# Decode attention over a key and value cache: values of pairs 0 to 12 issued by ScalarE instead of SyncE

## The chip, the core and the metric

The kernel runs on one core of a Trainium2 chip. The core has four engines that compute (TensorE or PE for matrix products, VectorE or DVE, ScalarE or ACT, GpSimd or POOL), SyncE (SP), which here only issues transfers, and 16 DMA engines that move data between the memory of the chip (HBM) and the memory of the core (SBUF, 128 partitions). Every engine works through its own list of instructions in order; semaphores tie the lists together. A transfer is issued by an instruction in the list of one engine, which puts it into that engine's DMA queue. The metric is the time of one execution on the device in microseconds (us), lower is better.

## The reference

One token is decoded. The cache holds 8192 keys and values for each of 32 heads, 128 numbers (float32) to a row, so that keys and values are 134 MB each.

```python
def _A_ref(x, k_cache, v_cache, wq, wo):            # x: [1, 1, 512]
    q = (x @ wq).reshape(B, Sq, H, Dh).transpose(0, 2, 1, 3)   # H = 32, Dh = 128
    scores = jnp.einsum("bhqd,bhkd->bhqk", q, k_cache) * (Dh ** -0.5)
    p = _softmax(scores, axis=-1)                   # over Sk = 8192
    o = jnp.einsum("bhqk,bhkd->bhqd", p, v_cache)
    return o.transpose(0, 2, 1, 3).reshape(B, Sq, H * Dh) @ wo
...
xn = _layernorm(x, axis=-1)
s = _A_ref(xn, A_k_cache, A_v_cache, A_wq, A_wo)
g = _silu(_B_ref(xn, B_w_gate, B_w_up, B_w_down))   # a gated layer, 512 -> 1376 -> 512
return x + s * g
```

## The kernel before

**Tiling.** The heads are worked in 16 pairs (`NP`). The keys of one pair are 8 MB and lie on 128 partitions, 64 for each head, as rows of 128 keys of 128 numbers (64 KB to a partition); the values likewise. SBUF holds three such slots: keys use `slots[0]` and `slots[1]` in turn (`slots[(i + 1) % 2]`), values always use `slots[2]`.

**One pair, in the order of its work.** VectorE multiplies the keys in place with the query of the head (L415) and sums each row (L416): these are the scores (`scores(i)`), and the step `summed[i]` marks their end. It then takes their largest (L418). TensorE turns these maxima to one row, VectorE reduces them (`all_max`, L408), TensorE spreads them, ScalarE makes the exponentials (`powers_of`, L428 and L430) and TensorE sums them. TensorE then multiplies weights and values in 64 matmuls (`pair`, L384 to L391) and raises `valued`; ScalarE copies the result out (`parts`, L437), TensorE picks the two heads from it and raises `picked`, and VectorE turns them (`heads_out`, L423).

**The loop over pairs (L440 to L458)** is written once per pair and fills the lists of all engines. VectorE's list holds, in this order, `all_max(i-1)`, `scores(i)`, `heads_out(i-1)`; ScalarE's holds `powers_of(i-1)`, `parts(i-1)`. TensorE runs `pair` in a loop, one pair after the other.

**Transfers.** All loads but one small one stand in SyncE's list, whose order is also the order of its DMA queue. `load_keys(i)` waits until VectorE has done the scores of pair i−2, which used the same slot (`summed[i - 2]`). `load_values(i - 1)` waits until TensorE has done the values of pair i−2 (`valued`). So SyncE's list reads K(2), V(1), K(3), V(2) and so on, with V(0) ahead of it, which waits for the end of the gated layer (`gated`). Each transfer of a full slot raises its own semaphore by 16 when it has landed. At the end SyncE's list has K(14), V(13), K(15), then the values of pairs 14 and 15 in parts, then the pieces of `wo`, which go to a key slot. The one load on ScalarE's queue is the row x (2 KB, L240).

**The end.** When the last pair is done, VectorE divides by the sums and turns the heads (`place`), and TensorE and VectorE share the product with `wo` (L507 to L539).

Of the kernel before, what the change touches and what calls it, by code (L numbers as in the profile page):

```python
# [51 lines left out]
def kernel(  # L52
# [19 lines left out]
    NP = H // 2  # L72
# [24 lines left out]
    DVE, ACT, SP, POOL = nc.vector, nc.scalar, nc.sync, nc.gpsimd  # L97
# [8 lines left out]
    def sb(name, *shape):  # L106
        return nc.alloc_sbuf_tensor(name, [P, *shape], F32)[:]
# [10 lines left out]
    slots = [sb(f"slot{i}", SLOT) for i in range(3)]  # L118
# [55 lines left out]
    def wait(eng, *steps):  # L174
        for s in steps:
            if s is not None:
                eng.wait_ge(*s)
# [24 lines left out]
    def rows_of(src, i):  # L202
        rows = src.rearrange("b h s d -> (b h s) d")[2 * i * S:2 * (i + 1) * S, :]
        return rows.rearrange("(p j) d -> p (j d)", p=P)
# [8 lines left out]
    def cols(j):  # L213
        return slice(j.start * Dh, j.stop * Dh)
# [5 lines left out]
            ld_k.setdefault(i, []).append((j, load(SP, f"k{n}_{j.start}", slots[n][:, cols(j)], rows_of(k_cache, i)[:, cols(j)])))  # L220

    def load_values(i, cut, *after):

        wait(SP, *after)
        for j in cut:
            sem = s_val[((0,) + V_CUTS).index(j.start)]
            SP.dma_start(slots[2][:, cols(j)], rows_of(v_cache, i)[:, cols(j)]).then_inc(sem, 16)  # L227

    load_keys(0, FULL)

# [138 lines left out]
    wait(PE, act(ACT.copy(s_gate, big[0])))  # L369
    gated = column_sums(big[1], s_gate)  # L370
    load_values(0, FULL, gated)
    wait(ACT, gated)
    c_sig = act(ACT.activation(g_row, big[1][:, :GC], AF.Sigmoid))
# [66 lines left out]
    for i in range(NP):  # L440
        if i > 0:
            all_max(i - 1)
        if i >= 2:
            load_keys(i, pieces(*K_CUTS.get(i, ())), summed[i - 2])
            if i < NP - 1:
                load_values(i - 1, FULL, (valued, i - 1))
        if i == NP - 1:
            for v, cut in ((i - 1, V_HALVES), (i, V_THREE)):
                load_values(v, cut[:1], (halved, v))
                load_values(v, cut[1:], (valued, v))  # L450
        scores(i)
        if i > 0:
            powers_of(i - 1)
            parts(i - 1)
            heads_out(i - 1)
        if i == 1:
            wait(DVE, c_sig)
            c_gate = dve(DVE.tensor_mul(g_row, g_row, big[1][:, :GC]))  # L458
# [81 lines left out]
    after = PE.take()  # L540
# [58 lines left out]
```

## Time and profile before

| | us |
|---|---|
| time, median of 3 runs | 684.8 (684.69 to 685.06) |
| the profiled execution's own time | 684.69 |
| its span, from the first to the last instruction | 683.3 |
| VectorE waited for keys, 8 times in all | 19.9 |
| keys, from issue to landing, median of the 13 full ones | 42.0 |
| values, from issue to landing, median of the 14 full ones | 29.3 |

The times of the views are those of the profiled execution, counted from the start of its span. In a row of the timeline the first number is the start and the second the length; then come engine, line, operation, what is written and read, and in brackets how long the engine had stood idle before and what ended that. A row of SPq or ACTq is an instruction that issues a transfer, so its length is that of the issue. The DMA view gives for each issue the time until the data had landed, and for each hardware queue its packets, its megabytes and its share of the time of 16 engines. In the windows view a row has, for each engine, busy time and number of instructions, then the granted clock of TensorE, the busy share of the DMA engines and GB/s. L38 stands for all instructions of TensorE, since a helper records them.

### The profile page before, as it was taken

How to read it: one execution, taken by the hardware profiler on the slowest of the kernel's cores; microseconds unless marked ns; L12 is line 12 of the kernel's file. 1: busy time of each engine (PE TensorE's matmuls, PEld its weight loads, DVE VectorE, ACT ScalarE, POOL GpSimd, SP SyncE). 2: the span in 40 equal slices, each digit the busy share in tenths (PEclk: the TensorE clock that was granted, in tenths of full speed). 3: DMA queues.
4: the chain of work that ended last, by engine and by line, in shares of the span. 5: the costliest groups of instructions: out<-in, count | busy, mean ns of one | idle time of the engine just before them, and what ended most of it. 6: DMA issues, size and time to landing. Idle time of an engine off the chain costs nothing. (4 is left out here: it accounts for less than half of the span.)

```text
span 683.3 us, 3400 instructions
## 1 busy us (share of the span) xinstructions
PE 218.8 (32%) x1376; PEld 62.3 (9%) x1376; DVE 616.0 (90%) x156; ACT 44.6 (7%) x142; POOL 2.6 (0%) x11
## 2 busy tenths in 40 slices
PE   0363025050503305050512306060512406060665
PEld 0120001010100101010100101010100101010110
DVE  3869999999999999998989899898989999999917
ACT  2040010000000100000010100000010101000010
POOL 0000000000000000000000000000000000000000
PEclk9987557575755757575665757575665757575897
DMA  9999999999999999999999999999999999999997
GB/s 382 429 440 460 437 434 430 430 430 430 430 430 430 430 430 430 460 441 445 434 430 430 430 430 430 430 430 430 430 437 437 460 430 403 472 399 430 435 430 331
DMA packets 7552, 293.67 MB, mean 430 GB/s; under 512 B 856, under 2 KB 864, under 8 KB 1664
## 3 DMA queue, kind: packets, MB, share of 16 engines
q1 hardware_dynamic: 7544, 293.67, 99.5%
q10 hardware_dynamic: 8, 0.00, 0.0%
HBM read 293.67 MB, written 0.00 MB: 430 GB/s over the span
## 5 line engine op out<-in xcount | busy, mean ns | idle before, releaser
L415 DVE TENSOR_TENSOR slot<-slot,q_all 128x16384 f32<-128x16384 f32 (+3 forms) x19 | 275.9, 14520 | 19.9 <-DMA slot<-in_A_k_cache_dram 19.9
L416 DVE TENSOR_REDUCE sc<-slot 128x128 f32<-128x16384 f32 (+3 forms) x19 | 276.0, 14525 | 0.7
L38 PE MATMUL psum<-slot,zeros 128*8 128x512 f32 x1024 | 148.5, 739 | 253.6 <-PEq L38 253.6
L38 PEld LDWEIGHTS psum<-slot,zeros 128*8 128x8 f32 x1024 | 30.3, 103 | 358.2 <-issue 358.2
L38 PE MATMUL psum<-ident,mx 128*1 128x128 f32 x32 | 8.4, 360 | 114.3 <-PEq L38 114.3
L437 ACT COPY o<-psum 128x512 f32<-128x512 f32 x16 | 9.4, 586 | 400.1 <-PE psum L38 400.1
L38 PE MATMUL psum<-slot,ones 128*128 (+3 forms) x36 | 17.7, 668 | 22.1 <-PEq L38 16.6
L290 DVE SCALAR_TENSOR_TENSOR slot<-slot,xn 128x1376 f32<-128x1376 f32 (+1 forms) x8 | 18.9, 2360 | 3.0 <-DMA slot<-in_A_wq_dram 2.7
L38 PE MATMUL psum<-o,pick 128*2 128x128 f32 x128 | 16.5, 272 | 12.8 <-PEq L38 12.8
L423 DVE STREAM_TRANSPOSE psum<-psum 32x128 f32<-32x128 f32 x16 | 5.0, 310 | 11.1 <-PE psum L38 11.1
L428 ACT ACTIVATE nb<-psum 128x2 f32<-128x2 f32 x16 | 2.8, 172 | 156.1 <-PE psum L38 156.1
L430 ACT ACTIVATE zeros<-sc,nb 64x128 f32<-64x128 f32 x32 | 12.8, 399 | 0.9
L38 PEld LDWEIGHTS psum<-ident,mx 128*1 128x1 f32 x32 | 1.8, 80 | 118.4 <-issue 118.3
L38 PEld LDWEIGHTS psum<-o,pick 128*2 128x2 f32 x128 | 9.9, 84 | 29.6 <-issue 27.2
L38 PE MATMUL psum<-slot,o_all 128*1 128x128 f32 (+1 forms) x54 | 9.5, 463 | 6.5 <-DMA slot<-in_A_wo_dram 6.5
L38 PE MATMUL psum<-zeros,rs 128*32 128x2 f32 x32 | 3.7, 187 | 23.5 <-PEq L38 23.5
L408 DVE TENSOR_REDUCE mx<-psum 1x2 f32<-1x128 f32 x16 | 4.4, 277 | 7.5 <-PE psum L38 7.5
L38 PE MATMUL psum<-mx,ones 1*128 1x2 f32 x32 | 8.2, 324 | 7.4 <-PEq L38 7.4
L515 DVE SCALAR_TENSOR_TENSOR q_all<-slot,o_all,q_all 128x512 f32<-128x512 f32 x15 | 10.0, 747 | 0.0
L38 PEld LDWEIGHTS psum<-slot,ones 128*128 128x128 f32 (+1 forms) x36 | 7.0, 218 | 32.5 <-issue 24.7
L38 PE MATMUL psum<-slot,o 128*1 128x512 f32 x26 | 5.0, 827 | 11.2 <-DMA slot<-in_B_w_down_dram 11.2
L38 PEld LDWEIGHTS psum<-mx,ones 1*128 1x128 f32 x32 | 7.3, 282 | 14.0 <-issue 14.0
(54 smaller groups left out, 61.3 us busy)
## 6 DMA issues: line engine op xcount, KB each, us to landing
slot<-in_A_k_cache_dram SPq DMA_DIRECT2D x2, 6144.0 KB, 37.9
slot<-in_A_v_cache_dram SPq DMA_DIRECT2D x3, 4096.0 KB, 23.0
slot<-in_A_wq_dram SPq DMA_DIRECT2D x2, 4096.0 KB, 16.6
slot<-in_A_k_cache_dram SPq DMA_DIRECT2D x2, 4096.0 KB, 40.5
slot<-in_A_k_cache_dram SPq DMA_DIRECT2D x2, 2048.0 KB, 42.4
slot<-in_B_w_gate_dram SPq DMA_DIRECT2D x1, 2752.0 KB, 26.9
slot<-in_B_w_up_dram SPq DMA_DIRECT2D x1, 2752.0 KB, 33.0
slot<-in_B_w_down_dram SPq DMA_DIRECT2D x1, 2560.0 KB, 22.7
```

What stands on the lines that cost most here:

```text
L38: ins = getattr(self.engine, name)(*args, **kwargs)
L290: return dve(DVE.scalar_tensor_tensor(y, w[:, k, cols], xn[:, k:k + 1], y, op0=ALU.mult, op1=ALU.add))
L408: DVE.reduce_max(mx[:1, 1:3], pt[0:1, :].rearrange("o (e p) -> o e p", e=2), axis=AX.X).then_inc(reduced, 1)
L415: wait(DVE, dve(DVE.tensor_mul(k[:, j, :], k[:, j, :], qb[:, i:i + 1, :].to_broadcast([P, n, Dh]))))
L416: summed[i] = dve(DVE.reduce_sum(sc[i % 2][:, j], k[:, j, :], axis=AX.X))
L423: turned_out[i] = dve(DVE.transpose(o, pn.rearrange("e (a r) -> e a r", r=WR)))
L428: wait(ACT, act(ACT.mul(nb, pm[:, :2], -SCALE)))
L430: ACT.activation(weights[h, :, e * HT:(e + 1) * HT], sc[i % 2][h].rearrange("p (g b) -> p g b", b=HT), AF.Exp, bias=nb[h, e:e + 1], scale= ...
L437: ACT.copy(o1, po).then_inc(copied, 1)
L515: ins = DVE.scalar_tensor_tensor(part[n], wo_t[:, r, :], col, part[n], op0=ALU.mult, op1=ALU.add)
```

## The change

The values of pairs 0 to 12 are issued by ScalarE, those of pairs 13 to 15 by SyncE as before. The waits are the same and move with the issues. In ScalarE's list the load of V(i−1) stands ahead of `powers_of(i-1)` and behind `parts(i-2)`; the first, V(0), stands ahead of the sigmoid of the gated layer (L373). SyncE's list keeps the keys, the weights and the end: K(2) to K(14) follow each other there with no values between them, then V(13), K(15) and the rest.

```diff
     def load_values(i, cut, *after):
-
-        wait(SP, *after)
+        eng = SP if i >= NP - 3 else ACT
+        wait(eng, *after)
         for j in cut:
             sem = s_val[((0,) + V_CUTS).index(j.start)]
-            SP.dma_start(slots[2][:, cols(j)], rows_of(v_cache, i)[:, cols(j)]).then_inc(sem, 16)
+            eng.dma_start(slots[2][:, cols(j)], rows_of(v_cache, i)[:, cols(j)]).then_inc(sem, 16)
```

## The prediction

> **What bounds the kernel now.** I read the page's header first, then its DMA lines, then the windows by stage.
>
> ```profile
> span 683.3 us, 3400 instructions
> DMA  9999999999999999999999999999999999999997
> q1 hardware_dynamic: 7544, 293.67, 99.5%
> 0.00:3.00 3.00, 0.00 (x0) 0.00 (x0) 0.17 (x1) 0.00 (x0) 0.99 (x8) 1.00 0.59 175
> 280.00:560.00 280.00, 80.31 (x546) 23.04 (x546) 258.93 (x37) 13.22 (x49) 0.00 (x0) 0.63 1.00 434
> ```
>
> The reader is to see that the 16 DMA engines, not VectorE, are the limit: one queue (q1, SP's) keeps them busy for 99.5% of the span, and the middle 280 us show a DMA share of 1.00 at 434 GB/s with VectorE at 259 of 280. So a change of order can gain almost nothing on the transfers; it can only lose, by leaving them without work. The question is what keeps them supplied. I write K(i) and V(i) for the loads of keys and values of pair i, S(i) for the end of its scores on VectorE, D(i) for the end of its value matmuls.
>
> ```profile
> 67.91 0.33 SPq L227 DMA_DIRECT2D slot<-in_A_v_cache_dram  x1
> slot<-in_A_v_cache_dram SPq DMA_DIRECT2D x1, 32.4
> 100.45 9.59 PE L38 MATMUL psum<-slot,zeros 128*8 128x512 f32 x64 [3.37 <-PEq L38]
> 370.97 9.15 PE L38 MATMUL psum<-slot,zeros 128*8 128x512 f32 x64 [20.01 <-PEq L38]
> 380.19 0.33 SPq L227 DMA_DIRECT2D slot<-in_A_v_cache_dram  x1
> 525.52 8.68 PE L38 MATMUL psum<-slot,zeros 128*8 128x512 f32 x64 [19.93 <-PEq L38]
> ```
>
> V(0), issued at 67.91, landed 32.4 later at 100.3; its matmuls start at 100.45. From there to those of pair 11 at 525.52 are 11 periods: 38.64 us each, two transfers of **19.32 us**. The values of pair 7 start at 370.97 and the next V, which waits for nothing else, is issued at 380.19: D is **9.2 us** after the landing's 0.1 (the whole group is 148.5 us for 16 pairs, 9.28).
>
> ```profile
> 312.87 17.23 DVE L415 TENSOR_TENSOR slot<-slot,q_all 128x16384 f32<-128x16384 f32 x1 [2.76 <-DMA slot<-in_A_k_cache_dram]
> 342.07 0.33 SPq L227 DMA_DIRECT2D slot<-in_A_v_cache_dram  x1
> slot<-in_A_v_cache_dram SPq DMA_DIRECT2D x1, 28.8
> 347.38 0.33 SPq L168 DMA_DIRECT2D slot<-in_A_k_cache_dram  x1
> slot<-in_A_k_cache_dram SPq DMA_DIRECT2D x1, 42.7
> ```
>
> Scores take 347.38 − 312.87 = **34.51 us**, and S(i) releases the slot for K(i+2), issued in the same instant. V lands 28.8 us after its issue: 9.5 us of waiting behind the K in transfer, then 19.3 at the full rate. That wait is the reserve. It covers the 9.2 us of matmuls in which the only value slot can take no load, and it exists because transfers are done whole, one after the other.
>
> **What the change does to each part.** Removed from SP: 13 value issues of 0.33 us and SP's waits for D. The K issues gain nothing by it: at 347.38 the K goes out with S(7) already now, and waits 23 us in its queue. The price of zero is covered by that. Added to ScalarE: 13 issues. The one issue that ScalarE makes before is the row of 1.08 us below; the SP row is 0.33. The wait for D(i−1) on ScalarE repeats the one it has in `parts` before its copy, so it holds nothing new; behind it stand the exponentials, whose first instruction came 2.83 us after D in the only place where PE's end decided (612.18 to 615.01, rows further below), so 1.08 is hidden.
>
> What decides is how the engines divide themselves between two queues. The trace of before has one place where two were filled: the x row (four rows of 512 B) on ScalarE's queue, beside 4 MB of wq on SP's.
>
> ```profile
> 0.74 1.50 SPq L168 DMA_DIRECT2D slot<-in_A_wq_dram  x2
> 2.38 1.08 ACTq L168 DMA_DIRECT2D x_row<-in_A_x_dram  x1
> DMA packets 18, 0.46 MB, mean 768 GB/s; under 512 B 0, under 2 KB 4, under 8 KB 4
> q1 hardware_dynamic: 14, 0.46, 176.9%
> q10 hardware_dynamic: 4, 0.00, 1.1%
> ...
> q1 hardware_dynamic: 3, 0.10, 28.4%
> ...
> DMA packets 19, 0.49 MB, mean 614 GB/s; under 512 B 4, under 2 KB 4, under 8 KB 4
> q1 hardware_dynamic: 15, 0.49, 142.1%
> q10 hardware_dynamic: 4, 0.00, 0.3%
> 13.16 2.35 DVE L289 TENSOR_SCALAR slot<-slot,xn 128x4096 f32<-128x4096 f32 x1 [0.58 <-DMA slot<-in_A_wq_dram]
> ```
>
> These are the DMA view's answers for 7.0 to 7.6, 7.6 to 8.4 and 8.4 to 9.2 us. q10 moves its four data packets in the first, none in the second, its four completion packets (under 512 B) in the third; between them q1 had its turn of about 1.2 us, which is one 32 KB piece, and its transfer was complete only at 13.16. So the queues are served **piece by piece in turn**. The Trainium skill, "DMA: Bandwidth & Descriptors", section "Queues, rings and completion order", says instead that an engine drains a whole packet, typically 9 to 17 descriptors, before it switches; eight pieces and a completion are nine, so by that rule whole transfers would alternate and the change would cost about nothing. This trace does not agree: its turn here is one piece.
>
> K and V have pieces of equal size (128 rows of 64 KB, eight per engine), so while both are under way each gets half. A V that met a K used to wait 9.5 and then run at full rate; now both run at half.
>
> Next, what couples D to VectorE: `heads_out(i-1)` stands behind `scores(i)` and waits for pair i−1. Once, this is seen to decide:
>
> ```profile
> 612.18 0.59 ACT L437 COPY o<-psum 128x512 f32<-128x512 f32 x1 [32.17 <-PE psum L38]
> 613.98 0.32 DVE L423 STREAM_TRANSPOSE psum<-psum 32x128 f32<-32x128 f32 x1 [0.35 <-PE psum L38]
> 614.41 8.67 DVE L415 TENSOR_TENSOR slot<-slot,q_all 128x8192 f32<-128x8192 f32 x1
> 615.01 0.17 ACT L428 ACTIVATE nb<-psum 128x2 f32<-128x2 f32 x1 [2.24 <-PE psum L38]
> ```
>
> The copy marks D = 612.18; the next scores start 2.23 us later. So when D is late, S = D + 2.23 + 34.51.
>
> Two terms no row shows alone: f, from S to the first bytes of K on an idle engine, and u, from D to the first bytes of V. For f: the first load of all is issued at 0.74, and in 0 to 3 us the DMA share is 0.59, 1.8 us of work, so bytes ran from about 1.2 on; bounds 0.33 (the issue alone) and 2.0, taken 1.0. For u: 0.4 (issue as on SP) to 5.0 (x row: issue at 2.38, packets after 7.0, with pieces of wq ahead), taken 2.5 between them.
>
> **The sum.** In the settled state a period P contains: V seen at D+u, landing after L, matmuls until the next D: P = u + L + 9.3. K is seen at D + 2.23 + 34.51 + 1.0 = D + 37.74, which is P + u − 37.74 ahead of the next V; that lead it has alone, and the rest is shared, so L = 38.64 − (P + u − 37.74). Adding, u drops out: 2P = 38.64 + 37.74 + 9.3 = 85.68, **P = 42.84** on the mean of two pairs, against 38.64: the DMA engines idle 4.2 us per pair.
>
> ```profile
> 92.13 0.33 SPq L168 DMA_DIRECT2D slot<-in_A_k_cache_dram  x1
> ```
>
> The start, by the same rules: S(0) = 92.13 (the issue of K(2)), and undisturbed pairs are 35.8 apart (two rows below). K(1) transfers from 100.3 − 38.64 = 61.7 on. V(0) is seen at 67.9 + 2.5 = 70.4 and slows it: K(1) has 8.7 of 19.3 done, the rest takes twice 10.6, and it lands at 91.5 instead of 81; VectorE wants it at 92.13 + 1.27 = 93.4, a cover of 1.9 us. Carried on so (before: 100.3 + 38.64 n):
>
> | pair n | V lands (before) | D | S(n) | engines idle after V or K |
> |---|---|---|---|---|
> | 0 | 107.5 (100.3) | 116.8 | 92.1 | 0 |
> | 1 | 149.0 (138.9) | 158.3 | 127.9 | 2.5 |
> | 2 | 195.5 (177.6) | 204.8 | 163.7 | 1.1 |
> | 3 | 239.1 (216.2) | 248.4 | 199.5 | 3.4 |
> | 4 | 281.2 (254.9) | 290.5 | 241.5 | 5.0 |
> | 5 | 324.8 (293.5) | 334.1 | 285.1 | 3.4 |
>
> From pair 4 on S follows D(n−2); gaps of 5.0 and 3.4 alternate to pair 11, and D(12) = 248.4 + 4 × 85.68 + 42.1 = 633.2. V(13) is again SP's, ahead of K(15), and waits for D(12): the engines are empty from V(12)'s landing at 623.9 to 634.2, 10.3 us. Idle in all: 2.5 + 1.1 + 5 × 3.4 + 4 × 5.0 + 10.3 = **50.9 us**.
>
> ```profile
> 574.08 0.33 SPq L227 DMA_DIRECT2D slot<-in_A_v_cache_dram  x1
> slot<-in_A_v_cache_dram SPq DMA_DIRECT2D x1, 28.6
> 613.35 0.29 DVE L418 TENSOR_REDUCE mx<-sc 128x1 f32<-128x128 f32 x1
> 649.15 0.29 DVE L418 TENSOR_REDUCE mx<-sc 128x1 f32<-128x128 f32 x1
> 660.98 1.89 PE L38 MATMUL psum<-slot,zeros 128*8 128x512 f32 x12 [0.89 <-PEq L38]
> 666.93 0.88 DVE L513 TENSOR_SCALAR q_all<-slot,o_all 128x512 f32<-128x512 f32 x2 [1.43 <-DMA slot<-in_A_wo_dram]
> ```
>
> The tail by transfers: V(13) landed at 574.08 + 28.6 = 602.7, 80.6 before the end; now 634.2 + 19.3 + 80.6 = 734.1. The tail by VectorE: S(14) = 633.2 + 36.74 = 669.9, S(15) 35.8 later (613.35 to 649.15) = 705.7, and from S(15) to the end 34.15 less the two waits for data that then vanish (0.89 and 1.43): **737.6**, the later one. The profiled execution took 684.69 with a span of 683.3, so 1.4 lies outside; its time is 0.1 under the median of 684.8. Predicted: **739.0 us**.
>
> **Rivals.** (1) **Whole transfers alternate**, the other side: K, V, K, V at full rate as now, V's reserve of 9.5 us stays, and the time is 684.8. It decides from turns of eight pieces on. The x row speaks against, though with small packets: 0.06. (The rule of the Trainium skill named above, "DMA: Bandwidth & Descriptors", would give this one.) (2) **Turns of about four pieces**, by deeper fetching from one queue: V is then served in blocks and part of the gaps go; between 0 and 54 us, about 712: 0.07. (3) **Two queues move more than one**: by the equation, two transfers of T each give 2P = 2T + 47.04, so P falls below 38.64 only if T is under 15.1 us, 28% more than 434 GB/s; then VectorE's 35.8 per pair sets the end: 92.1 + 15 × 35.8 + 31.9 + 1.4, about 662. The share of 1.00 at a constant rate speaks against: 0.03. (4) **V starts later still**, u at 5 and beyond: it is no longer cancelled, as K then has landed before V is seen, and the end is 760 or more: beyond 765 0.06. The forecast itself, 715 to 765: 0.78 (matmuls of 8.6 or 9.8 instead of 9.2 give 734 or 745, f from 0.33 to 2.0 gives 739 or 741, u from 0.4 to 5.0 gives 735 to 761). The range takes it and half of (2): 705 to 765. Within 0.2% (what a measurement here can tell from no change) 0.06, faster 0.03, slower 0.91.
>
> **What would show it.** Two hardware queues of which ScalarE's carries about 109 MB; a DMA share near 0.90 in the middle with holes of 3 to 5 us; value matmuls 42 to 44 us apart; V and K each landing 29 to 36 us after issue; VectorE before L423 waiting for PE in most pairs, where now only K is waited for; one hole of 10 us before V(13). Wrong is the step of turns if the share stays 1.00, and the step of coupling if L423 does not wait.

## The result and the profile after

| | before | after |
|---|---|---|
| time, median | 684.9 us (684.69 to 685.06) | **742.0 us** (740.88 to 746.2) |
| span of the profiled execution | 683.3 us | 739.7 us |
| ratio | | 1.0844 (95% interval 1.0826 to 1.0863) |

The change makes the kernel 57 us slower; the forecast was 739.0 in a range of 705 to 765. Where executions of one kernel lie over 1.5% apart, as in two of the experiments below, the ratio, if one is given, is that of the faster ones alone. The page of the changed kernel, its header, DMA lines and the two groups of VectorE that matter (busy us, mean ns, then idle time ahead of the group and what ended it):

```profile
span 739.7 us, 3400 instructions
...
DMA  9999999999999996999789896998969899599997
...
q1 hardware_dynamic: 5672, 184.62, 58.9%
q10 hardware_dynamic: 1880, 109.05, 34.1%
...
L415 DVE TENSOR_TENSOR slot<-slot,q_all 128x16384 f32<-128x16384 f32 (+3 forms) x19 | 275.7, 14510 | 0.0
...
L423 DVE STREAM_TRANSPOSE psum<-psum 32x128 f32<-32x128 f32 x16 | 5.1, 316 | 95.4 <-PE psum L38 95.4
```

The same bytes (184.62 + 109.05 = 293.67 MB) now go through two queues, and the DMA engines are no longer full. They were busy for 99.5% of 683.3 = 679.9 us; now for 58.9% + 34.1% of 739.7 = 687.9 us. So of the 56.4 us that the span grew, **48.4 us are time without work** (51.8 against 3.4) **and 8.0 us are longer packets**; the shares are rounded, which leaves about 1 us open between the two. VectorE waited 19.9 us for keys before; now it never waits for keys and waits 95.4 us for TensorE at L423. Read alone, that last line points at TensorE. The timeline of the changed kernel says what TensorE waited for:

```profile
281.15 9.52 PE L38 MATMUL psum<-slot,zeros 128*8 128x512 f32 x64 [26.89 <-PEq L38]
...
286.59 0.33 SPq L168 DMA_DIRECT2D slot<-in_A_k_cache_dram  x1
...
290.74 0.33 ACTq L227 DMA_DIRECT2D slot<-in_A_v_cache_dram  x1
...
292.54 0.32 DVE L423 STREAM_TRANSPOSE psum<-psum 32x128 f32<-32x128 f32 x1 [5.66 <-PE psum L38]
...
327.90 8.33 PE L38 MATMUL psum<-slot,zeros 128*8 128x512 f32 x64 [32.78 <-PEq L38]
```

The values are done at 290.74 and V(5) is issued in that instant; the matmuls that need it start at 327.90, 37.2 us later, for a transfer of 19.3 us. K(7) went out 4.15 us ahead of it. The DMA view of the same stretch, first for 290.74 to 295.2, then for one microsecond each from 295.2, 302.7, 305.1 and 307.5:

```profile
DMA packets 26, 1.70 MB, mean 382 GB/s; under 512 B 0, under 2 KB 0, under 8 KB 0
q1 hardware_dynamic: 26, 1.70, 88.3%
...
q10 hardware_dynamic: 16, 1.05, 242.0%
...
q1 hardware_dynamic: 15, 0.98, 226.8%
...
q10 hardware_dynamic: 15, 0.98, 226.8%
...
q1 hardware_dynamic: 15, 0.98, 227.0%
```

A packet is counted where it starts, and a 64 KB piece takes 2.42 us. For 4.5 us after its issue V gets nothing; then the 16 engines start a piece of V within 0.8 us of each other, 2.4 us later a piece of K, then V, then K, to the end of K. The queues are read in turn, one piece at a time. Between such shared stretches lie holes; the windows view (busy time of PE, PEld, DVE, ACT and POOL, clock, DMA share, GB/s):

```profile
283.00:285.00 2.00, 2.00 (x16) 0.33 (x8) 2.00 (x1) 0.00 (x0) 0.00 (x0) 0.50 0.00 0
...
240.00:600.00 360.00, 97.03 (x702) 27.66 (x702) 284.55 (x44) 17.00 (x63) 0.00 (x0) 0.63 0.91 386
600.00:660.00 60.00, 12.44 (x90) 3.57 (x94) 53.85 (x9) 1.89 (x7) 0.00 (x0) 0.59 0.85 364
```

From 283 to 285 TensorE works on values that have landed, VectorE on keys that have landed, and no transfer is under way: the value slot is being read and both key slots are full. In the middle the share is 0.91 where it was 1.00.

### The profile page after: what moved, and what is told of

Its sections match the earlier page's. It is cut to its first block, busy times and chain, and to the rows that moved or that the text cites. A ratio compares the mean times of both kernels' runs of the same rounds, so it can differ in the third digit from the quotient of the medians.

```text
span 739.7 us, 3400 instructions
## 1 busy us (share of the span) xinstructions
PE 212.1 (29%) x1376; PEld 60.6 (8%) x1376; DVE 615.2 (83%) x156; ACT 44.6 (6%) x142; POOL 2.6 (0%) x11
## 2 busy tenths in 40 slices
DMA packets 7552, 293.67 MB, mean 397 GB/s; under 512 B 856, under 2 KB 864, under 8 KB 1664
## 3 DMA queue, kind: packets, MB, share of 16 engines
q1 hardware_dynamic: 5672, 184.62, 58.9%
q10 hardware_dynamic: 1880, 109.05, 34.1%
HBM read 293.67 MB, written 0.00 MB: 397 GB/s over the span
## 5 line engine op out<-in xcount | busy, mean ns | idle before, releaser
L38 PE MATMUL psum<-slot,zeros 128*8 128x512 f32 x1024 | 146.2, 735 | 383.6 <-PEq L38 383.6
L423 DVE STREAM_TRANSPOSE psum<-psum 32x128 f32<-32x128 f32 x16 | 5.1, 316 | 95.4 <-PE psum L38 95.4
L38 PE MATMUL psum<-mx,ones 1*128 1x2 f32 x32 | 6.6, 273 | 7.4 <-PEq L38 7.4
L311 ACT COPY q_all<-psum 64x256 f32<-64x256 f32 x16 | 5.9, 367 | 20.6 <-PE psum L38 20.0
L38 PEld LDWEIGHTS psum<-mx,ones 1*128 1x128 f32 x32 | 5.7, 221 | 12.7 <-issue 12.7
L38 PEld LDWEIGHTS psum<-ident,mx 128*1 128x1 f32 x32 | 2.4, 83 | 52.4 <-issue 51.8
```

Source lines behind the costliest of these rows:

```text
L38: ins = getattr(self.engine, name)(*args, **kwargs)
L311: ins = ACT.copy(qb[h, 2 * t:2 * t + 2, :], q[h, :, e, :])
L423: turned_out[i] = dve(DVE.transpose(o, pn.rearrange("e (a r) -> e a r", r=WR)))
```

## The experiments

Four theories were held against each other. **A**, of the prediction: pieces in turn, so that V loses half its rate to a K that is early, and the loops of keys and values share one period. **B**: two queues move fewer bytes, or issues from ScalarE cost something. **C**: the late start of V is the loss. **D**: VectorE and the keys have slack, so their timing is of no account.

| kernel | time, us | ratio (95%) |
|---|---|---|
| keys in halves, two queues | 712.3 | 1.0400 (1.0383 to 1.0417) |
| keys in halves, one queue | 685.9 | 1.0014 (1.0004 to 1.0024) |
| keys in quarters, two queues | 701.8 | 1.0251 (1.0234 to 1.0268) |
| values later, two queues | 748.8 | 1.0935 (1.0880 to 1.0989) |
| keys later, two queues | 783.2 | 1.1433 (1.1377 to 1.1489) |
| keys later, one queue | 685.1 | 1.0003 (0.9992 to 1.0013) |
| half of the sums, two queues | 723.4 (718.2 and 728.7) | 1.0561 (1.0472 to 1.0650) |
| half of the sums, one queue | 684.9 | 0.9997 (0.9987 to 1.0008) |
| scores longer, two queues | 723.8 to 754.4 | 1.0570 (1.0548 to 1.0591) |
| scores longer, one queue | 699.7 | 1.0223 (1.0206 to 1.0240) |
| values of pairs 0 to 6 on ScalarE | 713.6 and 724.5 | |
| keys after values, two queues | 722.3 | 1.0542 (1.0524 to 1.0561) |

**The size of a turn.** If a turn is one piece, cutting the keys' pieces gives V a larger part without changing bytes, queues or issues of V.

```diff
-            ld_k.setdefault(i, []).append((j, load(SP, f"k{n}_{j.start}", slots[n][:, cols(j)], rows_of(k_cache, i)[:, cols(j)])))
+            m = j.start + NB // 2
+            for h in ((slice(0, m), slice(m, NB)) if j == slice(0, NB) else (j,)):
+                ld = load(SP, f"k{n}_{j.start}", slots[n][:, cols(h)], rows_of(k_cache, i)[:, cols(h)])
+            ld_k.setdefault(i, []).append((j, ld))
```

For the quarters the full load is cut into four in the same way.

> Two queues as in the changed kernel, but each full load of keys is two loads of 4 MB, so that its pieces are 32 KB and those of the values stay 64 KB; VectorE still waits for both halves. Theory A (the engines take one piece from each queue in turn, so a V that meets a K gets half the rate, and now would get two thirds): most of the loss goes, 688 to 702 us, holes between transfers nearly gone. Theory B (two queues on the same engines move less, or ScalarE's issues come late): 740 us or more, since bytes, queues and issues are the same and the pieces are smaller.

> The kernel before, one queue, with each full load of keys as two loads of 4 MB. Theory A: the size of pieces matters only for the turns between queues, so 684 to 687 us. Were smaller pieces faster as such, it would be under 683.

> Two queues, each full load of keys as four loads of 2 MB, so that keys go in pieces of 16 KB against 64 KB of the values, which then get four fifths while both are under way. Theory A with the start of V measured at 4 to 5 us: V takes 19.3 x 5/4 = 24.2, the loop of values is 4.5 + 24.2 + 9.3 = 38.0 per pair, under the 38.6 of the transfers: 690 to 706 us. Theory B (two queues move less): no better than 712, the time with halves.

The windows view of the keys in halves, then of the keys in quarters, then rows of the timeline of the quarters:

```profile
240.00:600.00 360.00, 93.53 (x642) 26.46 (x646) 316.48 (x48) 16.41 (x62) 0.00 (x0) 0.61 0.96 413
```

```profile
240.00:600.00 360.00, 104.94 (x706) 30.05 (x706) 330.52 (x52) 17.49 (x66) 0.00 (x0) 0.63 1.01 434
```

```profile
100.42 17.23 DVE L418 TENSOR_TENSOR slot<-slot,q_all 128x16384 f32<-128x16384 f32 x1 [9.02 <-DMA slot<-in_A_k_cache_dram]
...
294.24 17.23 DVE L418 TENSOR_TENSOR slot<-slot,q_all 128x16384 f32<-128x16384 f32 x1 [2.90 <-DMA slot<-in_A_k_cache_dram]
...
562.65 12.94 DVE L418 TENSOR_TENSOR slot<-slot,q_all 128x12288 f32<-128x12288 f32 x1
```

With a turn of 32 KB against 64 the DMA share rises from 0.91 to 0.96, with 16 KB it is full at the 434 GB/s of one queue. The starts of the packets show the turns themselves: while both are under way, a piece of V starts every 4.8 us in the changed kernel, every 3.6 us with the halves and every 3.0 us with the quarters, which is one piece of V and one of K each time. What is left of the loss, 17 us, has another form: now the keys are the ones that are slowed. K(1) beside V(0) comes 9.0 us late, and VectorE waits 2.9 us for keys from pair 2 on, where before it ran at its own 35.8 per pair up to pair 5 and had that lead at the end. Its scores of pair 13 start at 562.65 instead of 541.87, and VectorE ends last, by itself. On one queue the halves change 0.14%. That excludes theory B as the main cost: two queues can move all that one does. The expectation for the halves was missed, though: 712.3 against 688 to 702. It had taken V to start 1 to 2 us after D. In this run V's first packets come about 3.7 us after its issue (2.6 to 4.1), so V's own loop is 3.7 + 19.3 × 3/2 + 9.3 = 42.0, and the value matmuls of pairs 7 and 9 are 42.4 apart per pair, (470.49 − 385.63) / 2. In the pairs before, V is not shared over its whole length and the issues of V are 38.3 to 42.7 us apart.

```profile
385.63 9.53 PE L38 MATMUL psum<-slot,zeros 128*8 128x512 f32 x64 [30.38 <-PEq L38]
...
470.49 9.76 PE L38 MATMUL psum<-slot,zeros 128*8 128x512 f32 x64 [29.07 <-PEq L38]
```

With a start of 4 to 5 us put in, the quarters came out inside their range; they start 3.3 to 3.5 us after issue there, and the loss that is left, by late keys, was not part of that expectation.

**The start of V, the start of K.** One wait each, moved by a little.

```diff
-                load_values(i - 1, FULL, (valued, i - 1))
+                load_values(i - 1, FULL, (picked, i - 1) if i <= NP - 3 else (valued, i - 1))
```

```diff
-            load_keys(i, pieces(*K_CUTS.get(i, ())), summed[i - 2])
+            load_keys(i, pieces(*K_CUTS.get(i, ())), summed[i - 2], (turned, i - 1))
```

> The load of V(i-1) on ScalarE waits for the picking of heads of pair i-2 instead of for its values, about 1.9 us later, for V(1) to V(12). Theory A (the two loops share one period, in which the start of V cancels out, 2P = 38.6 + 37.7 + 9.3): the period of 43.1 stays within 0.4 us, time 741 to 749 us. Theory C (the late start of V is the loss): 12 x 1.9 = 23 us more, 765 us.

> The loads of keys on SyncE wait for one more step: K(i) for the turning of the maxima of pair i-2 on TensorE, which follows the values of pair i-3 there; in the changed kernel that is some 8 us after S(i-2). Keys land there 20 us before VectorE starts on them and it never waits for them. Theory A (the lead of K over the next V is what shortens V's shared transfer): without the lead the period grows by 2 to 6 us, 760 to 800 us. Theory D (keys have slack, VectorE's waits are for TensorE alone): no change, 740 to 746 us.

> The kernel before, one queue, with the loads of keys waiting for the turning of the maxima of pair i-2. There S(i-2) comes after the values of pair i-3, so it is 0.6 us, and K waits 23 us in the queue: 684 to 686 us by theory A, while in the changed kernel the same wait costs much.

Values later, the ends of pairs 3 and 11 on ScalarE (the copy starts when the values are done):

```profile
253.28 0.59 ACT L437 COPY o<-psum 128x512 f32<-128x512 f32 x1 [39.56 <-PE psum L38]
...
599.23 0.58 ACT L437 COPY o<-psum 128x512 f32<-128x512 f32 x1 [37.16 <-PE psum L38]
```

Eight periods of 43.24, against 43.11 in the changed kernel (249.88 to 594.77): V issued 1.8 us later in each of them, and the period is the same within 0.2. Theory C, with 765 us, falls: the kernel takes 6.8 us more than the changed one, and most of that lies outside these eight periods (in the profiled executions pair 3 is done 3.4 us later, and 2.6 us come behind pair 11). In the period the start of V does cancel out, since a later V finds more of K done. Keys later, the groups of VectorE and the middle:

```profile
L415 DVE TENSOR_TENSOR slot<-slot,q_all 128x16384 f32<-128x16384 f32 (+3 forms) x19 | 275.7, 14511 | 0.0
...
L423 DVE STREAM_TRANSPOSE psum<-psum 32x128 f32<-32x128 f32 x16 | 5.1, 317 | 135.9 <-PE psum L38 135.9
```

```profile
240.00:600.00 360.00, 85.10 (x624) 24.66 (x624) 258.81 (x40) 15.11 (x56) 0.00 (x0) 0.61 0.81 346
```

VectorE still never waits for a key (0.0), yet the kernel loses 41 us more: V and K now start together, V gets half the rate over its whole length, and the period is (577.61 − 291.05) / 6 = 47.8:

```profile
291.05 8.77 PE L38 MATMUL psum<-slot,zeros 128*8 128x512 f32 x64 [34.64 <-PEq L38]
...
577.61 8.85 PE L38 MATMUL psum<-slot,zeros 128*8 128x512 f32 x64 [34.44 <-PEq L38]
```

In the kernel before, the same wait costs nothing that can be told from zero (the interval holds 1). Theory D falls for keys.

**VectorE's turn.** Two ways, one shorter and one longer. The shorter one leaves out half of the sums; the scores that are not summed are set to zero beforehand.

```diff
+            j = slice(j.start, j.start + n // 2)
             summed[i] = dve(DVE.reduce_sum(sc[i % 2][:, j], k[:, j, :], axis=AX.X))
```

```diff
+            f = slice(j.start, j.start + n // 8)
+            wait(DVE, dve(DVE.reduce_sum(sc[i % 2][:, f], k[:, f, :], axis=AX.X)))
             summed[i] = dve(DVE.reduce_sum(sc[i % 2][:, j], k[:, j, :], axis=AX.X))
```

> VectorE sums the rows of only the first half of each piece of keys (the other half of the scores stays zero), so that its scores take 8.6 us less per pair; VectorE waited 95 us in the changed kernel. Theory A (VectorE's scores are one of the two turns in 2P, though it stands idle): P falls by half of 8.6 to the 38.6 of the transfers, 690 to 706 us. Theory B (transfers lose rate on two queues): 735 to 743 us, VectorE only waits longer.

> The kernel before, one queue, with the sums of the second half of each piece of keys left out: VectorE is 8.6 us shorter per pair. Theory A: transfers bound it, 682 to 685 us, VectorE waits for keys instead.

> Two queues as in the changed kernel; VectorE sums 16 of the 128 columns of each pair twice, about 2.2 us more per pair before the slot of the keys comes free. Theory A (half of each us of VectorE goes into the period, though VectorE waits 95 us in all): period 43.1 + 1.1 = 44.2, over nine periods 10 us, and 2 to 4 us in the last pairs: 751 to 758 us. Theory D (VectorE's idle time hides it): only the last pairs, 742 to 747 us.

> The kernel before, one queue, with the same sums twice. VectorE waited 2 to 3 us per pair for keys from pair 6 on, and the reserve covers the rest: all theories 684 to 690 us.

Half of the sums gains 19 us on two queues (13 and 24 in its two executions), where VectorE waits 95 us, and nothing on one, where it waits for keys instead (the group of L417 there):

```profile
L417 DVE TENSOR_TENSOR slot<-slot,q_all 128x16384 f32<-128x16384 f32 (+3 forms) x19 | 276.0, 14527 | 90.5 <-DMA slot<-in_A_k_cache_dram 90.5
```

So VectorE's scores are in the loop that theory A names, and theory B would have shown no gain. But the gain is 19 us where 36 to 52 were expected: the period fell to 41.9, (508.09 − 256.96) / 6 by the ends of pairs 3 and 9, not to 38.6:

```profile
256.96 0.59 ACT L440 COPY o<-psum 128x512 f32<-128x512 f32 x1 [44.54 <-PE psum L38]
...
508.09 0.58 ACT L440 COPY o<-psum 128x512 f32<-128x512 f32 x1 [45.50 <-PE psum L38]
```

With 8.6 us off, in every second pair the next K is issued before the V in transfer has landed (K(8) at 319.09, while V(5) lands at 331.1) and takes turns from it a second time, which the equation leaves out; it holds near the state for which it was set up, not that far from it.

The longer scores have by far the widest scatter. Their five executions took 723.8, 724.0, 734.5, 743.5 and 754.4 us. So the time came out as neither theory had it (A 751 to 758, D 742 to 747), and three of the five lie under the 742.0 of the changed kernel although VectorE has more to do. The profiled one is that of 743.5, with a span of 741.4. In its trace, L425 is the turning of heads (L423 before):

```profile
321.47 0.32 DVE L425 STREAM_TRANSPOSE psum<-psum 32x128 f32<-32x128 f32 x1
...
369.74 0.32 DVE L425 STREAM_TRANSPOSE psum<-psum 32x128 f32<-32x128 f32 x1 [10.53 <-PE psum L38]
...
590.79 0.32 DVE L425 STREAM_TRANSPOSE psum<-psum 32x128 f32<-32x128 f32 x1 [5.42 <-PE psum L38]
```

Up to 321 VectorE waits for nothing; from 369.74 on it waits in every pair, and the period is (590.79 − 369.74) / 5 = **44.2**, the 43.1 + 1.1 that was expected, in this one execution. It got there at pair 6 and not at pair 3, and was ahead of the changed kernel until then: the values of pair 3 are done at 234.39, against 249.88. This fits VectorE, at 38.1 us per pair, running ahead of the transfers' 38.6 far more slowly than at 35.8, so that the holes begin later; but the first holes, at 275.1 and 316.5, come before VectorE's first wait, and what sets them off wasn't followed. That a run's time depends on when the holes begin would fit the scatter; only one execution has a profile, so it isn't shown. By its times alone this run speaks for none of the four theories. The one-queue expectation was simply wrong: it forgot that VectorE had only 2.9 us to give, and at 38.1 per pair from S(0) on it ends at 92 + 15 × 38.1 + 34, near the measured 697.

**How long, and in which order.**

```diff
-        eng = SP if i >= NP - 3 else ACT
+        eng = SP if i >= 7 else ACT
```

> Values of pairs 0 to 6 on ScalarE's queue, 7 to 15 on SyncE's. Theory A (holes per pair with two queues, and nothing to win back as the transfers are the bound with one): about 22 us for the start up to D(3) and 4.5 for each further pair, less what the reserve takes in again, 706 to 718 us. Were the loss at the start or at the hand-over alone, it would be 735 or more, or under 700.

```profile
240.00:380.00 140.00, 42.47 (x310) 12.06 (x310) 106.81 (x18) 6.60 (x24) 0.00 (x0) 0.64 0.86 367
400.00:600.00 200.00, 63.90 (x442) 17.97 (x438) 185.24 (x27) 9.44 (x35) 0.00 (x0) 0.64 1.00 434
```

Of its two executions 713.6 lies in the range and 724.5 above it; the profile is that of the first. The windows view has a share of 0.86 from 240 to 380, which takes in the hole of 10 us at the hand-over (from 368 on), and 1.00 from 400 on with one queue again. So the holes end with the second queue, and the loss stays. The last kernel adds a wait to the changed one, so that a K starts when a V has ended:

```diff
                 taken(s_val[((0,) + V_CUTS).index(j)], 16)
+                if j == 0:
+                    PE.nop().then_inc(arrived, 1)
...
-            load_keys(i, pieces(*K_CUTS.get(i, ())), summed[i - 2])
+            load_keys(i, pieces(*K_CUTS.get(i, ())), summed[i - 2], (arrived, i - 1) if i < NP - 1 else None)
```

> Two queues; one wait is added. K(i) on SyncE, i up to 14, waits for S(i-2) and also until TensorE has taken V(i-2) as landed, so that the next K starts when a V has ended and is ahead of the next V by the time of the matmuls and of V's start, some 13 us, instead of by 5 us and 10 us in turn. Theory A: V then runs 38.6 - 13 = 25 us, the hole per pair is one start of a transfer, 1 to 2 us; period 39.6 to 40.6, time 700 to 718 us, 25 us or more under the changed kernel though a wait is added and nothing is taken away. Theories B, C and D (fewer bytes per us on two queues, late values, waits that only add): 742 us or more.

The groups of VectorE, with `L418` the multiplication and `L426` the turning of heads, and the value matmuls of pairs 7 and 9:

```profile
L418 DVE TENSOR_TENSOR slot<-slot,q_all 128x16384 f32<-128x16384 f32 (+3 forms) x19 | 276.0, 14524 | 60.0 <-DMA slot<-in_A_k_cache_dram 60.0
...
L426 DVE STREAM_TRANSPOSE psum<-psum 32x128 f32<-32x128 f32 x16 | 4.9, 309 | 10.2 <-PE psum L38 10.2
```

```profile
391.09 8.97 PE L38 MATMUL psum<-slot,zeros 128*8 128x512 f32 x64 [13.36 <-PEq L38]
...
474.07 8.44 PE L38 MATMUL psum<-slot,zeros 128*8 128x512 f32 x64 [13.31 <-PEq L38]
```

A wait is added, nothing is removed, keys come so late that VectorE waits 60 us for them, and the kernel is **20 us faster** than the changed one (722.3 against 742.0): the period is 41.5. It is 4 us over the range expected, as 2.9 us per pair are added to the 38.6 of the transfers, where 1 to 2 were expected: a hole of 2.0 us and slow first packets behind it (see the end). None of these is faster than the kernel before, whose DMA engines have 3.4 us left to gain.

## Why the prediction was right, point by point

- **The bound.** The DMA engines were full and could only lose. Right: on two queues they move the same 434 GB/s at best (keys in quarters).
- **Turns of one piece**, read from the x row. Right, and now shown for full transfers in the DMA windows. By the Trainium skill, "DMA: Bandwidth & Descriptors", section "Queues, rings and completion order", a whole packet of typically 9 to 17 descriptors is drained before a switch; these traces do not agree, a turn was one piece of 64 KB in the changed kernel, and with smaller pieces V's share grew as such turns would have it. The Trainium skill, "DMA: Bandwidth & Descriptors", section "Issuing engines are not separate DMA queues", states that transfers of different engines run on the same DMA engines and interleave; the rows from 295.2 to 307.5 agree with it, where 15 or 16 pieces of V and of K start by turns 2.4 us apart.
- **The coupling at L423.** Right: 95.4 us of waits for TensorE, in 12 pairs.
- **The period.** Forecast 42.84; measured (594.77 − 249.88) / 8 = 43.11, by the ends of pairs 3 and 11:

```profile
249.88 0.59 ACT L437 COPY o<-psum 128x512 f32<-128x512 f32 x1 [42.27 <-PE psum L38]
...
594.77 0.59 ACT L437 COPY o<-psum 128x512 f32<-128x512 f32 x1 [38.93 <-PE psum L38]
```

  The alternation was there too, but three to four times as large: pairs of 40.9 and 45.6 to 46.7 (the last 43.5) where 42.1 and 43.6 were forecast, and holes of 6 to 7.4 and of about 1.4 us where 5.0 and 3.4 were forecast. The equation fixes only the mean of two pairs; why the swing is larger wasn't followed.
- **The start.** Values of pairs 0 to 5 begin at 105.06, 148.65, 194.49, 240.39, 281.15 and 327.90; forecast landings were 107.5, 149.0, 195.5, 239.1, 281.2 and 324.8.
- **The sum.** 50.9 us idle were forecast, 48.4 more than before were measured. D(12) was forecast at 633.2 and came at 636.23:

```profile
636.23 0.33 SPq L227 DMA_DIRECT2D slot<-in_A_v_cache_dram  x1
...
slot<-in_A_v_cache_dram SPq DMA_DIRECT2D x1, 21.8
...
724.28 0.88 DVE L513 TENSOR_SCALAR q_all<-slot,o_all 128x512 f32<-128x512 f32 x2
```

  V(13) landed 21.8 after its issue, so it had the engines to itself, as forecast; the hole ahead of it was about 8.4 us, forecast 10.3; and at 724.28 VectorE no longer waits for `wo`, so VectorE's tail is the later one.
- **Mis-sized terms.** u, the start of V, was taken as 2.5. With a K under way V's first packets come 3.6 to 5.1 us after issue, 4.6 in the median; on idle engines after 0.95, as for V(13). The size did little harm because it cancels; in the expectation for keys in halves, where it doesn't cancel, it did. Rival (4) had it cancel no longer from a u of 5 on, with 760 us or more; in values later V's packets start about 6 us after D, and the period stayed at 43.24 with 748.8 us, so that price was too high. f was taken as 1.0 and is 0.95 (K(7)), but the reading behind it was wrong: the DMA share counts a packet where it starts, and in the kernel before none starts ahead of 1.7 us, where the prediction had bytes from 1.2 on. Left out of the sum were the longer packets, 8.0 us. The tail of VectorE, 3.5 us behind the transfers in the forecast, is in fact about level with them: TensorE waits for `wo` until 735.59, 4 us before the end.
- **Luck.** The forecast span was 683.3 + 54.3 (50.9 idle, the rest the tail); measured were 56.4, of which 8.0 are packets that were in no term. That the total came within 3 us is in part luck, since the idle time and the tail were taken somewhat too long; the mean period is where the mechanism was met.

## What to carry to other kernels

When one queue already keeps the DMA engines full, its order is a schedule: it gives each transfer the full rate when its turn comes, and waiting in it is a reserve. Here a second queue did not add bandwidth, it divided it, so the transfer with the shortest time to spare pays for one that is early. Before splitting, ask which load has a single buffer behind it, and if two queues are wanted anyway, give that load the larger pieces, which here took the loss from 57 to 17 us. And an engine that waits is not off the loop: VectorE waited 95 us, and 8.6 us less of its work per pair still gained 19 us.

## What the runs showed of the hardware

- A turn is counted in pieces, not in bytes: pieces of 64 KB against 64, 32 and 16 KB gave 742.0, 712.3 and 701.8 us, with a piece of V every 4.8, 3.6 and 3.0 us.
- The completion of a transfer takes a turn of its own. K(7)'s last pieces start near 317.4; windows of the changed kernel from 319.3 to 320.4 and from 322.1 to 322.9:

```profile
q10 hardware_dynamic: 16, 1.05, 220.3%
...
DMA packets 24, 0.79 MB, mean 983 GB/s; under 512 B 12, under 2 KB 12, under 8 KB 12
q10 hardware_dynamic: 12, 0.79, 226.7%
q1 hardware_dynamic: 12, 0.00, 0.8%
```

  Between them each engine moves one more piece of V, so K lands 2.4 us after its last byte. The completion packets of the x row had shown it before, and the prediction had not priced it.
- A transfer issued while the other queue is busy gets its first packet late: 3.6 to 5.1 us after issue in the changed kernel, 2.6 to 4.1 with keys in pieces of 32 KB, 3.3 to 3.5 in pieces of 16 KB, 4.9 for the x row (issued at 2.38, first packet at 7.26). On idle engines it is 0.95 us on either queue. What the time consists of isn't known.
- The engines' busy time grew by 8.0 us for the same bytes. In the packet records most of it lies in 144 pieces of 64 KB that take about 3.1 us instead of 2.42, mostly the first of a K after a hole. In keys later, where V is the one that starts after the hole, nearly all such pieces are V's; with keys in quarters, where the middle has no hole, there are none. So it goes with the hole and not with the queue. Why the first is slow isn't known.
